# Split products from the sixth hidden block on, and low halves of w_out formed on GpSimd, in an attention and two-MLP kernel

## The chip, the cores and the metric

The kernel runs on one core of a Trainium2 chip. The number that counts is the device time of one execution in microseconds (us). Before the change three runs gave 1339.31, 1339.48 and 1341.15 us, so the median is 1339.48 us. Five engines work side by side: TensorE (PE in the profile, its weight loads PEld), VectorE (DVE), ScalarE (ACT), GpSimd (POOL) and SyncE (SP, which here only starts transfers).

## The reference

A small attention between 512 tokens and 32 state rows is computed in each of 8 batches and 8 heads. Its 4352 result rows of 512 values go through two MLPs, the first with a smooth step, the second with a sloped ReLU:

```
g  = where(h >= 1, h, where(h <= -1, 0, (h + 1)**2 / 4))   # h = x @ w_in,  512 -> 2048
x1 = g @ w_out                                             # 2048 -> 512
g2 = max(h2, 0) + alpha * min(h2, 0)                       # h2 = x1 @ w_in2
out = g2 @ w_out2
```

The weights arrive as 64-bit floats and are turned into 32-bit floats on the chip.

## The kernel before, in words

The first MLP runs over nine tiles of tokens: eight tiles of 512 tokens, one for each batch, and a last one of 256 state rows. Within a tile the 2048 hidden units are taken in 16 blocks of 128. A step `i` of the main loop stands for one tile and one block (step 0 to 15 is the first tile). It writes, in this order, the first layer of step i+2 (`h_mm`), the side work listed for that step in a table (`at(i, ...)`), the activation (`act_fn`, which forms `g`), the high and low half of the next step's `g` (`g_split`), and the second layer of step i (`out_mm`, four sums `accA` of 128x512). A scheduler then settles the order in which the instructions of each engine stand in the program.

A product of two 32-bit matrices is taken in one of two ways. In the whole form (line 602) it is one f32 matmul, which the trace shows as two passes. In the split form (line 610, and line 85 for the first layer, `hA`) both factors are cut into a high half, rounded to type `fp32r` by ScalarE (`hi_`, line 74), and the low rest, which VectorE forms by a subtraction (`lo_`, line 77). The product is then three fp32r matmuls: high by high, high by low and low by high. `NAT = 9` (line 100) says that steps 0 to 8 take their second layer in the whole form and all later steps in the split form.

The weight block `f` of w_out must therefore be there in the whole form by step f, and in two halves by the first step that uses the split form. `decode` turns 64-bit words into f32: one operation on ScalarE (`dec0`, line 372) and four on VectorE (`dec1`, lines 383 to 391). `dec_hi` makes the high half and `dec2` the low one; before the change blocks 9 to 15 get their halves in the first tile, blocks 0 to 8 only when the second tile comes to them.

During the first tile the program also prepares what the other tiles need. TensorE makes products of state and w_in in pairs of 64 rows each (`vg_mm`, line 481, `vgp`); ScalarE copies them out (`vgo`, line 484); GpSimd moves some of them to other partitions by DMA (`v0_move`, line 492) into `vr`, which ScalarE and VectorE split into `vw` for the first layer of the first tile; and GpSimd stores the decoded w_in in DRAM (`wi_store`, line 439, 64 transfers). VectorE also decodes w_in and does parts of the second batch's softmax. The PSUM tiles of `vgp`, of `hA` and of the attention scores come from one pool of four banks, so a `vgp` waits until an older tile of the pool has been read. All engines run their own instructions in the order in which they stand.

Of the kernel before, what the change touches and what calls it, by code (L numbers as in the profile page):

```python
# [40 lines left out]
def kernel_body(ctx: ExitStack, tc: tile.TileContext, x, state, w1i, w1o, w2i, w2o, alpha, out):  # L41
# [22 lines left out]
    act, dve, pool, pe, ld = nc.scalar, nc.vector, nc.gpsimd, nc.tensor, nc.sync  # L64
# [11 lines left out]
    def lo_(l, raw, h, eng=None):  # L76
        (eng or dve).tensor_tensor(out=l, in0=raw, in1=h.bitcast(F32), op=ALU.subtract)  # L77
# [19 lines left out]
    w2d = dp.tile([8, 7, 128, 512], F32, name="w2d")  # L97
    wd = [dp.tile([DM, 512], F32, name=f"wd{k}") for k in range(4)]
    GRP = [(1, 2, 3, 4), (0, 5, 6, 7)]
    NAT = 9  # L100


    A = {}
# [256 lines left out]
    G = {}  # L360
# [39 lines left out]

    def dec2(key):
        h, l = W[key]
        lo_(l, G.pop(("dec", key)), h)

    def decode(key, o):
        at(o - 1, dec0, key)
        at(o, dec1, key)
# [107 lines left out]
    def src_w1o(f):  # L515
        return w1o[f * 128:(f + 1) * 128, :]
# [20 lines left out]
    def gi(t, f):  # L537
        return t * NF + f
# [41 lines left out]
    def g_split(i):  # L580
        n = wd_(steps[i][0])
        g = GG.pop(i)
        if i < NAT:
            GH[i] = g
# [7 lines left out]
    def out_mm(i):  # L592
        t, f = steps[i]
        n = wd_(t)
        if f == 0:
            for k in range(NO):
                ACC[k] = pa.tile([128, 512], F32, tag="acc", name=f"accA{t}{k}")
        if i < NAT:

# [441 lines left out]
    def at(i, fn, *a):  # L1041
        side[i].append((fn, *a))
# [23 lines left out]
    for b in range(1, NB):  # L1066
        t0 = gi(b - 1, 0)
        for q in range(2):
            o = t0 + (2 if b > 1 else 5)
# [22 lines left out]
        for blk in range(4):  # L1092
            for q in range(2):
                o = t0 + 10 + 4 * blk + q
# [5 lines left out]
    for blk in (1, 2, 3):  # L1100
        for c in range(4):
            o = 4 * blk - 7 + c - (blk > 1)
# [2 lines left out]
            decode(("wi", blk, c), o)  # L1105
    at(1, vdirect, 0, 1)
    for f in range(1, NF):
        o = f - 2 - (f >= NAT)
        if f > 2:
            at(o - 3, d_load, ("w1o", f), src_w1o(f))  # L1110
        decode(("w1o", f), o)
    for f in range(NF):
        o = gi(1, f - 3) if f < NAT else f - 2
        at(o, dec_hi, ("w1o", f))
        at(o + 1, dec2, ("w1o", f))
    for n in range(4):
        at(n - 4, vg_mm, 1 - n % 2, 0, 2 + n // 2)
        at(n - 2, vg_store, 1 - n % 2, 0, 2 + n // 2)
# [1 line left out]
    for blk in range(4):  # L1120
        for c in range(4):
            if blk:
                o = 4 * blk - 3 + c
                at(o, vg_mm, 0, blk, c)
                at(o + 2, vg_store, 0, blk, c)
                o = 13 + c if blk < 2 else 4 * blk - 7 + c
# [142 lines left out]
```

## Time and profile before

| what | us |
|---|---|
| median of three runs (lowest, highest) | 1339.48 (1339.31, 1341.15) |
| profiled execution, its own time | 1339.59 |
| span of that execution in the trace | 1337.8 |
| TensorE busy in the span | 1327.5 |
| VectorE, ScalarE, GpSimd busy | 1025.7, 764.3, 186.9 |
| mean granted clock of TensorE | 0.999 of full speed |

The time of an execution is its span and a little around it, 1.8 us here. A busy time sums up what an engine did, and says nothing about who waited for whom at one place. That is read from the chain of waits, which is followed back from the last instruction, and from the instructions in order of time. Where a row of those carries a bracket, the engine was idle before it, and the bracket says for how long and what ended the wait. Durations of VectorE overlap a little with the next one: an operation of 0.69 us is followed by the next after 0.60 us.

### The profile page before, as it was taken

To read this page: it belongs to the slowest core of one execution; us is meant where nothing else is said; L and a number is where in the kernel's file an instruction comes from. 1 tells how busy PE (TensorE), PEld (TensorE's weight loads), DVE (VectorE), ACT (ScalarE), POOL (GpSimd) and SP (SyncE) were. 2 spreads that over 40 slices of the span, in tenths; PEclk is the share of its full clock that TensorE was granted. 3 is DMA by queue.
4 is the path that set the end of the run, shared out by engine and by line. 5 is a ranking of instruction groups with operands and counts; after the bars stand their busy time and mean duration, and the time that the engine had idled before them with its cause. 6 is when DMAs were issued, how large, how long until landed. Compare 5 with 4: busy or idle time off the path is not lost.

```text
span 1337.8 us, 21107 instructions
## 1 busy us (share of the span) xinstructions
PE 1327.5 (99%) x6962; PEld 1109.2 (83%) x6962; DVE 1025.7 (77%) x1868; ACT 764.3 (57%) x1500; POOL 186.9 (14%) x284
## 2 busy tenths in 40 slices
PE   9999999999999999999999999999999999999998
PEld 5335688878878888888988888888899999999998
DVE  6978575978697879776978696777868877796875
ACT  5757765666576666666745453554625445562543
POOL 1015400232323332223311000000000000000000
PEclk9999999999999999999999999999999999999999
DMA  8978862564666674465566865866688888969876
GB/s 278 328 268 235 244 144 66 129 191 125 205 157 191 172 233 141 144 227 174 204 221 221 283 205 173 266 186 212 212 269 265 285 273 299 310 209 298 272 255 191
DMA packets 262828, 293.03 MB, mean 219 GB/s; under 512 B 145152, under 2 KB 149824, under 8 KB 262720
## 3 DMA queue, kind: packets, MB, share of 16 engines
q1 hardware_dynamic: 243968, 247.73, 59.9%
q0 software_dynamic: 11904, 34.65, 7.3%
q10 hardware_dynamic: 6848, 9.31, 2.0%
q8 instruction: 56, 0.92, 0.3%
q14 instruction: 52, 0.43, 0.1%
HBM read 224.47 MB, written 66.06 MB: 217 GB/s over the span
## 4 chain that ended last, share of the span: by engine, by line
PE 92%; DVE 3%; issue 2%; ACT 2%; DMA 1%; POOL 1%; SPq 0%; ACTq 0%; DVEq 0%; POOLq 0%
PE accA L610 25%; PE accB L863 24%; PE hB L784 22%; PE hA L85 13%; PE accA L602 2%; PE vgp L481 2%; DMA x<-in_x_dram 1%; DMA vr<-vgo 1%; PE sr L253 1%; PE sc L159 1%; DVE c L810 0%; PE et L235 0%; ACT m L795 0%; DVE c L797 0%; ACT vgo L484 0%
## 5 line engine op out<-in xcount | busy, mean ns | idle before, releaser
L863 PE MATMUL accB<-gs,wv 128*128 128x384 f32 (+1 forms) x1668 | 331.4, 357 | 0.0
L863 PEld LDWEIGHTS accB<-gs,wv 128*128 128x128 f32 x1668 | 298.6, 188 | 27.6 <-DVE gs L77 1.9
L784 PE MATMUL hB<-xh,wu 128*128 128x384 f32 (+1 forms) x1120 | 314.7, 357 | 0.2 <-ACT p L814 0.2
L784 PEld LDWEIGHTS hB<-xh,wu 128*128 128x128 f32 x1120 | 205.8, 188 | 19.3 <-ACT p L814 1.4
L784 PE MATMUL hB<-xl,wu 128*128 128x384 f32 (+1 forms) x560 | 199.6, 356 | 0.0
L795 ACT ACTIVATE m<-c 128x384 f32<-128x384 f32 (+1 forms) x120 | 68.2, 568 | 140.4 <-DVE c L810 138.9
L578 DVE SCALAR_TENSOR_TENSOR g<-y,hA 128x512 f32<-128x512 f32 (+1 forms) x144 | 93.8, 651 | 56.2 <-ACT y L576 55.6
L77 DVE TENSOR_TENSOR gl<-g,gh 128x512 fp32r<-128x512 f32 (+1 forms) x135 | 95.1, 704 | 42.0 <-ACT gh L74 40.5
L797 DVE SCALAR_TENSOR_TENSOR c<-m,beta_sb,c 128x384 f32<-128x384 f32 (+1 forms) x120 | 80.9, 674 | 59.8 <-ACT m L795 56.2
L575 ACT ACTIVATE y<-hA 128x512 f32<-128x512 f32 (+1 forms) x144 | 82.7, 575 | 66.7 <-PE hA L85 66.6
L77 DVE TENSOR_TENSOR gs<-c,gs 128x384 fp32r<-128x384 f32 (+1 forms) x200 | 113.3, 604 | 6.9 <-ACT gs L845 6.4
L784 PEld LDWEIGHTS hB<-xl,wu 128*128 128x128 f32 x560 | 105.1, 188 | 8.7
L74 ACT CAST gh<-g 128x512 fp32r<-128x512 f32 (+1 forms) x135 | 80.3, 595 | 47.2 <-DVE g L578 39.1
L845 ACT CAST gs<-c 128x384 fp32r<-128x384 f32 (+1 forms) x200 | 101.6, 554 | 9.0 <-PE accB L863 8.6
L576 ACT ACTIVATE y<-y 128x512 f32<-128x512 f32 (+1 forms) x144 | 87.5, 608 | 3.8
L837 DVE TENSOR_TENSOR c<-c,c 128x384 f32<-128x384 f32 (+1 forms) x120 | 71.9, 608 | 2.1
L676 POOL DMA_DIRECT2D w2d<-wo x72 | 50.6, 904 | 132.0 <-DVE wo L77 66.0
L906 ACT COPY o<-accB 128x384 f32<-128x384 f32 (+1 forms) x30 | 15.7, 525 | 79.5 <-PE accB L863 77.3
L676 POOL DMA_DIRECT2D w1d<-wu x56 | 38.4, 753 | 149.6 <-DVE wu L77 122.9
L810 DVE TENSOR_TENSOR c<-hB,u 128x384 f32<-128x384 f32 (+1 forms) x80 | 48.4, 605 | 13.6 <-PE hB L784 11.7
L77 DVE TENSOR_TENSOR gs<-m,gs 128x384 fp32r<-128x384 f32 (+1 forms) x80 | 46.5, 607 | 12.4 <-ACT gs L845 12.4
L484 ACT COPY vgo<-vgp 128x512 f32<-128x512 f32 x64 | 34.3, 591 | 28.8 <-PE vgp L481 28.2
(905 smaller groups left out, 2662.0 us busy)
## 6 DMA issues: line engine op xcount, KB each, us to landing
wu<-w1d SPq DMA_DIRECT2D x280, 256.0 KB
wv<-w2d SPq DMA_DIRECT2D x280, 256.0 KB
vr<-vd SPq DMA_DIRECT2D x56, 256.0 KB
w1d<-wu POOLq DMA_DIRECT2D x56, 256.0 KB, 5.3
w2d<-wo POOLq DMA_DIRECT2D x40, 256.0 KB, 5.5
x<-in_x_dram SPq DMA_DIRECT2D x16, 512.0 KB
wr_wi<-in_moe_w_in_dram SPq DMA_DIRECT2D x16, 512.0 KB
wr_w1o<-in_moe_w_out_dram SPq DMA_DIRECT2D x16, 512.0 KB
```

What stands on the lines that cost most here:

```text
L74: act.copy(h, raw)
L77: (eng or dve).tensor_tensor(out=l, in0=raw, in1=h.bitcast(F32), op=ALU.subtract)
L85: pe.matmul(ps, a, b, start=(k == 0), stop=(k == n - 1))
L575: act.activation(out=y[:, :n], in_=ps, func=AF.Relu, bias=0.5, scale=0.5)
L576: act.activation(out=y[:, :n], in_=y[:, :n], func=AF.Square)
L578: dve.scalar_tensor_tensor(out=g[:, :n], in0=y[:, :n], scalar=1.0, in1=ps, op0=ALU.min, op1=ALU.max)
L610: pe.matmul(ACC[k][:, :n], a, b, start=(f == 0 and j == 0), stop=(f == NF - 1 and j == 2))
L676: pool.dma_start(out=dst, in_=src)
L784: pin(pe.matmul(ps, a[:, kk], b, start=(new and m == 0), stop=(m == 5), skip_group_check=True))
L797: dve.scalar_tensor_tensor(out=g, in0=m, scalar=beta_sb[:, f:f + 1], in1=h, op0=ALU.mult, op1=ALU.add)
L845: tc.keep_in_program_order(act.copy(h, src))
L863: pin(pe.matmul(ps, a[:, js], b, start=(new and k == 0 and n == 0), stop=(k == 7 and n == 2), skip_group_check=True))
```

## The change

There are three edits. `NAT` becomes 5, so that steps 5 to 8 of the first tile take their second layer in the split form, too. `dec2` gives its subtraction to GpSimd instead of VectorE, for all 16 blocks of w_out of the first MLP. And the table is moved so that the halves of blocks 5 to 8 are made in the first tile: the high half one step before the block is used, the low half in the same step. Blocks 9 to 15 keep their places.

```diff
-    NAT = 9
+    NAT = 5
     def dec2(key):
         h, l = W[key]
-        lo_(l, G.pop(("dec", key)), h)
+        lo_(l, G.pop(("dec", key)), h, pool)
     for f in range(1, NF):
-        o = f - 2 - (f >= NAT)
+        o = f - 2 - (f >= 9)
     for f in range(NF):
-        o = gi(1, f - 3) if f < NAT else f - 2
+        o = gi(1, f - 3) if f < NAT else f - 2 + (f < 9)
         at(o, dec_hi, ("w1o", f))
-        at(o + 1, dec2, ("w1o", f))
+        at(o + (f < NAT or f >= 9), dec2, ("w1o", f))
```

The order of the program changes on TensorE in steps 5 to 8 and at one pair of the second tile (eight transposes move by four products there, too). The first place is the end of block 5 in the first tile, on TensorE, before the change; `vgp` is the pair of 64-row products, `hA` the first layer, `accA` a sum of the second layer.

```order
L602 MATMUL accA_568<-g_739,wf_w1o_665 128x512
L602 MATMUL accA_569<-g_739,wf_w1o_665 128x512
L481 MATMUL vgp_887<-wf_wi_0_715,sts_223 128x512
L481 MATMUL vgp_888<-wf_wi_0_715,sts_223 128x512
L85 MATMUL hA_898<-ath_548,vw020h 128x512
L85 MATMUL hA_898<-atl_549,vw020h 128x512
```

The same place after the change, on TensorE:

```order
L610 MATMUL accA_569<-gl_801,w_w1o_5h 128x512
L610 MATMUL accA_569<-gh_800,w_w1o_5l 128x512
L481 MATMUL vgp_911<-wf_wi_0_715,sts_223 128x512
L610 MATMUL accA_566<-gh_878,w_w1o_6h 128x512
L610 MATMUL accA_566<-gl_879,w_w1o_6h 128x512
L481 MATMUL vgp_912<-wf_wi_0_715,sts_223 128x512
L85 MATMUL hA_922<-ath_548,vw020h 128x512
L85 MATMUL hA_922<-atl_549,vw020h 128x512
```

The pair of 64-row products no longer stands together: two products of the next block, the second of which needs the low half `gl_879`, stand between its members. From block 5 to block 8 four pairs stand apart in this way after the change (`vgp_868`, `vgp_911`, `vgp_941`, `vgp_993` and the product after each), and two before it (`vgp_856` and `vgp_913`).

The second place is block 0 of the second tile, on TensorE, before the change:

```order
L610 MATMUL accA_1564<-gh_1488,w_w1o_0l 128x512
L610 MATMUL accA_1565<-gh_1488,w_w1o_0h 128x512
L610 MATMUL accA_1565<-gl_1489,w_w1o_0h 128x512
L610 MATMUL accA_1565<-gh_1488,w_w1o_0l 128x512
L481 MATMUL vgp_1578<-wf_wi_3_502,sts_223 128x512
L481 MATMUL vgp_1579<-wf_wi_3_502,sts_223 128x512
```

The same place after the change, on TensorE:

```order
L610 MATMUL accA_1627<-gh_1552,w_w1o_0l 128x512
L481 MATMUL vgp_1642<-wf_wi_3_502,sts_223 128x512
L610 MATMUL accA_1628<-gh_1552,w_w1o_0h 128x512
L610 MATMUL accA_1628<-gl_1553,w_w1o_0h 128x512
L610 MATMUL accA_1628<-gh_1552,w_w1o_0l 128x512
L610 MATMUL accA_1629<-gh_1552,w_w1o_0h 128x512
L610 MATMUL accA_1629<-gl_1553,w_w1o_0h 128x512
L610 MATMUL accA_1629<-gh_1552,w_w1o_0l 128x512
L481 MATMUL vgp_1643<-wf_wi_3_502,sts_223 128x512
```

Here, too, one pair now stands apart, with six products between its members.

The third place is VectorE at the end of the decoding for step 6, before the change; `wf` is a decoded weight block, and the `g` written here frees the bank of an `hA`.

```order
L391 SCALAR_TENSOR_TENSOR wf_w1o_848<-wr_w1o_721,wf_w1o_848 128x512
L391 SCALAR_TENSOR_TENSOR wf_w1o_850<-wr_w1o_723,wf_w1o_850 128x512
L578 SCALAR_TENSOR_TENSOR g_868<-y_869,hA_827 128x512
L77 TENSOR_TENSOR vw021l<-vr_766,vw021h 128x512
L383 TENSOR_SCALAR wf_wi_3_905<-wf_wi_3_905 128x512
```

The same place after the change, on VectorE:

```order
L391 SCALAR_TENSOR_TENSOR wf_w1o_856<-wr_w1o_721,wf_w1o_856 128x512
L391 SCALAR_TENSOR_TENSOR wf_w1o_858<-wr_w1o_723,wf_w1o_858 128x512
L77 TENSOR_TENSOR gl_879<-g_807,gh_878 128x512
L578 SCALAR_TENSOR_TENSOR g_883<-y_884,hA_835 128x512
L77 TENSOR_TENSOR vw021l<-vr_766,vw021h 128x512
L383 TENSOR_SCALAR wf_wi_3_929<-wf_wi_3_929 128x512
```

The low half of block 6's `g` stands in front of the next `g`; blocks 5, 7 and 8 gain one such row each, and the 16 subtractions for w_out leave the engine. On GpSimd they stand between its transfers: those of blocks 5 to 9 between the moves into `vr`, that of block 10 behind the last move, those of blocks 11 to 15 and 0 to 4 between the 64 stores of w_in.

## Rows read from the trace of the kernel before

**Rows 1.** The page: busy time by engine, and granted clock in tenths by slice
```profile
PE 1327.5 (99%) x6962; PEld 1109.2 (83%) x6962; DVE 1025.7 (77%) x1868; ACT 764.3 (57%) x1500; POOL 186.9 (14%) x284
...
PEclk9999999999999999999999999999999999999999
```

**Rows 2.** Stretch 72 to 112: length, then PE, PEld, DVE, ACT, POOL busy
```profile
72.00:112.00 40.00, 39.67 (x120) 15.75 (x121) 34.91 (x73) 26.53 (x51) 4.98 (x10) 1.00 0.74 245
```

**Rows 3.** Chain of waits in order of time: start, length, what
```profile
57.15 3.63 PE accA L602 x8
...
80.51 1.05 PE vgp L481 x2
81.56 1.05 PE accA L602 x2
...
83.67 2.77 PE accA L602 x6
...
96.82 1.59 PE hA L85 x6
...
119.21 1.06 PE vgp L481 x4
120.27 2.93 PE accA L610 x12
123.20 1.36 PE hA L85 x6
...
135.32 2.72 PE accA L610 x12
```

**Rows 4.** TensorE in order of time: start, length, engine, line, tile, idle before
```profile
80.44 1.12 PE L481 MATMUL vgp<-wf_wi,sts 64*128 64x512 f32 x2
...
86.37 1.55 PE L481 MATMUL vgp<-wf_wi,sts 64*128 64x512 f32 x4
...
113.03 1.13 PE L481 MATMUL vgp<-wf_wi,sts 64*128 64x512 f32 x4
114.09 0.50 PE L610 MATMUL accA<-gh,w_w1o_9h 128*128 128x512 f32 x1
...
117.98 0.50 PE L85 MATMUL hA<-ath,vw031h 128*128 128x512 f32 x1 [0.21 <-ACT vw031h L74]
```

**Rows 5.** VectorE in order of time, same columns
```profile
78.44 0.69 DVE L391 SCALAR_TENSOR_TENSOR wf_w1o<-wr_w1o,wf_w1o 128x512 int32<-128x512 int32 x1
79.58 0.45 DVE L383 TENSOR_SCALAR wf_wi<-wf_wi 128x512 f32<-128x512 f32 x1 [0.45 <-ACT wf_wi L372]
...
86.06 0.68 DVE L578 SCALAR_TENSOR_TENSOR g<-y,hA 128x512 f32<-128x512 f32 x1
...
89.20 0.44 DVE L383 TENSOR_SCALAR wf_wi<-wf_wi 128x512 f32<-128x512 f32 x1 [1.86 <-ACT wf_wi L372]
...
102.64 0.68 DVE L578 SCALAR_TENSOR_TENSOR g<-y,hA 128x512 f32<-128x512 f32 x1
...
106.85 0.68 DVE L77 TENSOR_TENSOR w_w1o_9l<-wf_w1o,w_w1o_9h 128x512 fp32r<-128x512 f32 x1
...
110.78 0.68 DVE L578 SCALAR_TENSOR_TENSOR g<-y,hA 128x512 f32<-128x512 f32 x1
```

**Rows 6.** All engines in order of time around 374, in a later tile
```profile
374.38 3.12 DVE L77 TENSOR_TENSOR gl<-g,gh 128x512 fp32r<-128x512 f32 x1
...
374.54 1.02 POOL L654 TENSOR_TENSOR sao<-wf_w2o,wf_w2o 128x256 f32<-128x256 f32 x1
...
375.93 1.02 POOL L654 TENSOR_TENSOR sao<-sao,wf_w2o 128x256 f32<-128x256 f32 x1
```

**Rows 7.** All engines in order of time around 403
```profile
402.89 0.73 POOL L654 TENSOR_TENSOR sao<-sao,wf_w2o 128x256 f32<-128x256 f32 x1
...
403.04 1.13 DVE L77 TENSOR_TENSOR gl<-g,gh 128x512 fp32r<-128x512 f32 x1 [0.69 <-ACT gh L74]
```

**Rows 8.** Groups by line on GpSimd: count, busy and mean, idle before
```profile
L439 POOL DMA_DIRECT2D wd<-wf_wi x64 | 31.4, 498 | 13.3 <-DMA wd<-wf_wi 10.0 <-DVE gl L77 2.7 <-DMA vr<-vgo 0.6
```

## The prediction

> **What bounds the kernel now.** The page comes first: TensorE is busy for 99% of the span at a granted clock of full speed, all other engines for 77% or less [rows 1]. So a change pays only where it shortens TensorE's own work, or ends one of its few waits, and costs only where it makes TensorE wait. The second view is the busy time by stretch, for the time in which steps 5 to 8 run: in the 40 us from 72 to 112 TensorE idles for 0.3 us, and VectorE, with 34.91 us of work, is nearer to its limit than anywhere its 77% would suggest [rows 2]. The reader is to see that this stage has two full engines, not one. The third view is the chain of waits, which here runs along TensorE and so gives the price of each piece of its work, and the fourth is TensorE and VectorE in order of time, which shows who waits for whom.
>
> **Prices on TensorE.** A second-layer block in the whole form takes 3.63 us; in the split form 2.93 us behind a `vgp`, and 2.72 us, 0.227 a product, behind a first layer [rows 3]. The first layer takes 1.36 us behind split products and 1.59 behind a `vgp`. That is the arithmetic that speaks for the change: 3.63 - 2.93 = 0.70 for each of four blocks, 2.8 us. But a `vgp` pair takes 1.06 us, and half a pair that stands alone takes 1.05: the two halves run side by side, and a half alone saves nothing. Before the change two pairs are torn apart, by pieces of the second layer of 1.05 and 2.77 us [rows 3]; after it four are, and one more in the second tile.
>
> **Edit 1, split form in steps 5 to 8: TensorE's own work.** Before, from the lone `vgp` at 80.44 on: steps 5 and 6 take 1.05 + 1.05 + 1.05 + 2.77 + 1.06 + 1.59 = 8.57 us each, steps 7 and 8 take 1.06 + 3.63 + 1.06 + 1.59 = 7.34 each; the sum is 31.8 us. After, the same stretch holds 48 second-layer and 24 first-layer products at 0.227, 16.3 us, and 12 visits to `vgp` work (four pairs torn into eight, four whole). A visit among split products costs 1.06 and the 0.21 that the next split piece is longer behind it, 1.27; twelve cost 15.2 us. The sum is 31.6 us, so the gain on TensorE is 0.2 us instead of 2.8: the torn pairs have eaten the rest. The torn pair in the second tile costs 1.27 us. The rest of TensorE's order is that of before, and no term comes from it.
>
> **Waits that go.** The stretch from 80.44 to the `vgp` at 113.03 lasted 32.59 us [rows 4], 0.8 more than the 31.8 of work; the pair at 86.37 that took 1.55 instead of 1.06 shows most of it (its second half waits until a `g` has been read out of a bank, the `g` at 86.06 [rows 5]). And from 114.09 to 117.98 the second layer and half a first layer take 3.89 us where 2.93 + 3 x 0.227 = 3.6 were work: TensorE waits for the moved `vr` and its high half [rows 4], 0.3 us, and 0.3 more for its low half behind it. If TensorE comes to that place later, these 0.6 us go, too.
>
> **Edit 2, low halves on GpSimd: what it costs VectorE.** On VectorE such a subtraction takes 0.60 us of its time (the 0.68 us row at 106.85, the next starting 0.60 later [rows 5]). No row shows it on GpSimd at 128x512; at 128x256 a subtraction took 0.73 us undisturbed [rows 7], so at twice the width it takes between 0.73 and 1.46 us, and I take 1.3, near the row's cost per element. What it does to VectorE is the disputed price. Three GpSimd subtractions from 374.54 to 376.95 held a VectorE subtraction for 3.12 us instead of 0.69, 2.4 us longer; one at 402.89 held another for 1.13, 0.44 longer [rows 6, 7]. So VectorE stands still while GpSimd works, for 0.6 to 1 of the GpSimd time where it wants to work at once. For one low half of 1.3 us that is 0.8 to 1.3 us; where VectorE happens to be at work that GpSimd doesn't touch, it is nothing. It can't be a gain in steps 5 to 8, because only one subtraction leaves VectorE there, that of block 9. I take 0.9 us for each of the five low halves (blocks 5 to 9) that fall into the stage, and keep 0 and 1.3 as bounds.
>
> The Trainium skill (SBUF — State Buffer, "SBUF: two separate sides") says that the shared port pair of the two engines is an exclusive lock for a whole instruction, against VectorE operations with two SBUF inputs or in a two-port mode. The trace agrees with it in the 3.12 us row [rows 6]. By that rule the decode steps of this stage, nearly all of that kind, would be stopped for the whole low half, the upper bound. The same skill (GPSIMD Engine Reference, "3.1 Elementwise — side-by-side cycle accounting") gives about 2.6 cycles an element, from which I estimate 1.1 us and a start-up for 512 columns; with that the sum would stay within the range.
>
> **New waits on TensorE.** VectorE ended the decode before step 5's at 79.04, 0.54 us ahead of the next one, which began at 79.58 and ran without a break to the `g` at 86.06 [rows 5], 6.48 us. Now it has the low half of block 5's `g` (0.60) and the stop by w_out's block 5 (0.9) before that, and starts at 80.54; 6.48 and the stop by block 6 later, at 87.9, comes the low half of block 6's `g`, ready at 88.5, then the next `g`, ready at 89.1. TensorE gets there at 80.44 + 1.05 + 1.12 + 1.05 + 2.03 + 1.05 and one product = 87.1. It waits 1.4 us for the low half and 0.3 us for the bank that the `g` frees, in front of the second half of the torn pair. In steps 6 and 7 VectorE waits for decodes of ScalarE, as at 89.20 where it idled for 1.86 us [rows 5]; ScalarE does those behind the copies of the torn pair, so they come later by what TensorE is late, and VectorE wins back little. By the same count the `g` of block 9, which began at 102.64, is ready at 106.7, and the first layer of block 10 waits for its bank for 0.5 us. From that `g` to the next one VectorE needed 8.14 us before (102.64 to 110.78 [rows 5]); it loses block 9's subtraction (0.60), gains a reduction of the softmax that slips behind the `g` (0.60) and the stop by block 9 (0.9). The next `g` is ready at 115.75. TensorE stands at 114.3 then and could end its pair at 115.4; its second half starts at 115.8 and the pair ends at 116.85, 1.5 us late. New waits: 1.7 + 0.5 + 1.5 = 3.7 us.
>
> **The sum.** -0.2 (own work) - 0.8 and - 0.6 (old waits) + 3.7 (new waits) + 1.27 (torn pair in the second tile) = +3.4 us. What else moves costs nothing: the casts of blocks 5 to 8 on ScalarE are the same in number and lie in its idle time (26.5 of 40 us busy [rows 2]); if that cover were gone, the copies behind them and a `vgp` would come 0.5 us later each. In the second tile VectorE has nine subtractions fewer, but TensorE waits for none of them. The profiled execution took 1339.59 us, 1.79 above its span and 0.1 above the median; with 3.4 it gives 1343.0, and the median of 1339.48 gives 1342.9. I say 1342.8.
>
> **Rivals.**
>
> GpSimd doesn't hinder VectorE: stops of 0. For it speaks that in other stages operations of VectorE pass by GpSimd work unhurt; against it the two rows just used. Then VectorE is late by the 0.6 us of each low half of `g` alone, the waits of 3.7 shrink to 0.4 at the last pair, and the sum is -0.2 - 0.8 - 0.6 + 0.4 + 1.3 = +0.1: 1339.5 us, not slower. It decides below a stop of 0.2 us; at 0.5 the sum is +1.7.
>
> Torn pairs cost nothing: half a pair runs beside the products around it. Then two more torn pairs in the first tile and the one in the second cost about 0.2 us instead of 3.4, and with no stops the time falls by some 3.5 us, to 1336. The lone half at 80.51 that took 1.05 us speaks against it [rows 3].
>
> GpSimd's own queue is late. Eleven low halves (block 10 on) stand among or ahead of its 64 stores, 14 us of work where the queue had idled for 13.3 us, mostly for earlier stores to end [rows 8]. Each low half is behind a fixed number of stores (that of block 13 behind 23 of them, that of block 2 behind 54), and buffers that ScalarE and VectorE need are freed by those stores. I count a margin of 2 to 4 us for the tightest; should stores take 6 instead of 4 us each round because VectorE is in the way, TensorE waits once for 3 us more, on top of the forecast: 1346.
>
> **How the numbers follow.** The forecast has a chance of 0.50, no hindrance 0.27, torn pairs at no cost 0.04, a late queue 0.19. About 0.2% of the time, 2.7 us, is what a measurement can tell from no change. The forecast's own range goes from +1.7 (stops of 0.5) to +4.8 (1.3), 1341.2 to 1344.3, and three fifths of it lie above 2.7 us. Slower: 0.30 + 0.19, and a little more for what I haven't found, 0.50. The same: 0.20 + 0.25, 0.45. Faster: 0.05. The range is 1339.0 to 1346.0: it takes in the case without stops and the late queue, and leaves out the rival that is faster.
>
> **What would show it.** Right: on TensorE, waits in front of the product with `gl` of block 6, of the second half of that torn pair, and of the second half of the pair ahead of block 9, released by VectorE; decode operations of VectorE of 1.3 us and more beside a low half on GpSimd; three more lone `vgp` halves of 1.05 us; everything behind 165 us moved by a constant. Wrong: low halves on GpSimd with VectorE's operations at their usual 0.42 and 0.69 us; a TensorE without waits from 80 to 120; or waits released by GpSimd, which would be the queue. The size would be wrong if a low half on GpSimd took under 0.8 us or over 1.6.

## The result

The change makes the kernel slower by 0.64%: six runs of the changed kernel had a median of 1346.76 us (1345.96 to 1352.43), six of the kernel before 1339.72 (1338.29 to 1342.02), the ratio is 1.0064 with a 95% interval of 1.0052 to 1.0076. The prediction was 1342.8 us, slower, with a range to 1346.0. The direction was right; the loss is about twice what was forecast. The profiled execution took 1345.99 us over a span of 1344.2, 6.4 us more than that of before.

Where these 6.4 us lie is read from TensorE's instructions in order of time, at five marks that both kernels have: the first `vgp` of step 5, the first products with blocks 9 and 10 of w_out in the first tile, and those with blocks 0 and 1 in the second.

| TensorE | before, us | after, us | difference | forecast |
|---|---|---|---|---|
| start to `vgp` of step 5 | 80.44 | 81.12 | +0.7 | 0 |
| steps 5 to 8, up to block 9's product | 33.65 | 37.39 | +3.7 | +2.7 |
| block 9's to block 10's product | 6.11 | 7.05 | +0.9 | -0.6 |
| block 10's to block 0's product | 31.07 | 31.06 | 0.0 | 0 |
| block 0's to block 1's product | 5.38 | 6.66 | +1.3 | +1.3 |
| from there to the end | 1181.2 | 1180.9 | -0.2 | 0 |

(The forecast's +2.7 is made of -0.2 own work, -0.8 of an old wait and +3.7 of new ones.)

### The profile page after: what moved, and what is told of

Read it like the earlier page. It is cut to its first block, busy times and chain, and to the rows that moved or that the text cites. A ratio compares the mean times of both kernels' runs of the same rounds, so it can differ in the third digit from the quotient of the medians.

```text
span 1344.2 us, 21197 instructions
## 1 busy us (share of the span) xinstructions
PE 1329.9 (99%) x6978; PEld 1113.3 (83%) x6978; DVE 1030.9 (77%) x1856; ACT 766.1 (57%) x1504; POOL 208.6 (16%) x300
## 4 chain that ended last, share of the span: by engine, by line
PE 89%; DVE 5%; issue 2%; ACT 2%; DMA 1%; POOL 1%; SPq 0%; ACTq 0%; DVEq 0%; POOLq 0%
PE accA L610 25%; PE accB L863 24%; PE hB L784 22%; PE hA L85 12%; PE vgp L481 1%; PE accA L602 1%; DMA vr<-vgo 1%; PE sr L253 1%; DMA x<-in_x_dram 0%; DVE c L810 0%; PE et L235 0%; PE sc L159 0%; DVE wf_w1o L388 0%; ACT m L795 0%; DVE c L797 0%
## 5 line engine op out<-in xcount | busy, mean ns | idle before, releaser
L77 DVE TENSOR_TENSOR gl<-g,gh 128x512 fp32r<-128x512 f32 (+1 forms) x139 | 100.4, 722 | 45.6 <-ACT gh L74 44.2
```

## The profile after

The page's first part and the stretch from 72 to 112 us, which answer to [rows 1, 2]; the columns are the same.

```profile
PE 1329.9 (99%) x6978; PEld 1113.3 (83%) x6978; DVE 1030.9 (77%) x1856; ACT 766.1 (57%) x1504; POOL 208.6 (16%) x300
```

```profile
72.00:112.00 40.00, 37.04 (x126) 17.52 (x127) 36.44 (x64) 27.97 (x54) 12.53 (x15) 1.00 0.67 228
```

The page's first part could be taken for that of before: shares of 99 and 77% again. The stretch can't. TensorE, which idled for 0.3 us there, now idles for 3.0, and VectorE, with fewer instructions in the same 40 us than before (64 for 73), is busy for longer (36.44 for 34.91 us). An instruction takes it 0.57 us in the mean instead of 0.48.

GpSimd and VectorE of the changed kernel in order of time say why (start, length, engine, line, tile, idle before). First GpSimd:

```profile
74.69 1.46 POOL L77 TENSOR_TENSOR w_w1o_5l<-wf_w1o,w_w1o_5h 128x512 fp32r<-128x512 f32 x1 [0.95 <-ACT w_w1o_5h L74]
...
93.46 1.84 POOL L77 TENSOR_TENSOR w_w1o_7l<-wf_w1o,w_w1o_7h 128x512 fp32r<-128x512 f32 x1 [0.93 <-ACT w_w1o_7h L74]
...
116.51 1.43 POOL L77 TENSOR_TENSOR w_w1o_10l<-wf_w1o,w_w1o_10h 128x512 fp32r<-128x512 f32 x1
117.88 2.96 POOL L439 DMA_DIRECT2D wd<-wf_wi  x6
120.85 1.41 POOL L77 TENSOR_TENSOR w_w1o_11l<-wf_w1o,w_w1o_11h 128x512 fp32r<-128x512 f32 x1
```

Then VectorE:

```profile
74.62 0.42 DVE L385 TENSOR_SCALAR wf_wi<-wf_wi 128x512 int32<-128x512 int32 x1
74.95 1.49 DVE L385 TENSOR_SCALAR wf_w1o<-wf_w1o 128x512 int32<-128x512 int32 x1
...
88.67 0.68 DVE L77 TENSOR_TENSOR gl<-g,gh 128x512 fp32r<-128x512 f32 x1
...
94.08 1.50 DVE L385 TENSOR_SCALAR wf_w1o<-wf_w1o 128x512 int32<-128x512 int32 x1
...
116.72 0.68 DVE L578 SCALAR_TENSOR_TENSOR g<-y,hA 128x512 f32<-128x512 f32 x1
117.32 0.90 DVE L383 TENSOR_SCALAR wf_w1o<-wf_w1o 128x512 f32<-128x512 f32 x1
...
119.45 1.67 DVE L391 SCALAR_TENSOR_TENSOR wf_w1o<-wr_w1o,wf_w1o 128x512 int32<-128x512 int32 x1
121.04 1.78 DVE L77 TENSOR_TENSOR gl<-g,gh 128x512 fp32r<-128x512 f32 x1
122.74 0.67 DVE L578 SCALAR_TENSOR_TENSOR g<-y,hA 128x512 f32<-128x512 f32 x1
123.33 0.68 DVE L77 TENSOR_TENSOR vw031l<-vr,vw031h 128x512 fp32r<-128x512 f32 x1
```

The two operations of line 385 at 74.62 and 74.95 are the same work; the second, beside a subtraction of GpSimd, takes 1.49 us instead of 0.42, a stop of 1.07. The same is seen beside block 7 (1.50, a stop of 1.08). Beside blocks 6, 8 and 9 one operation each time was longer by 1.0, 1.0 and 1.4 us. Beside block 10 it is 0.48 (0.90 for 0.42), and the `g` at 116.72, one of whose operands is in PSUM, isn't stopped at all. Beside block 11 two operations are stopped, by 1.0 and 1.1 us (1.67 and 1.78 against 0.69); the first lies ahead of the row of GpSimd's subtraction, whose times are rough.

TensorE in order of time, which answers to [rows 4]:

```profile
89.40 0.49 PE L610 MATMUL accA<-gl,w_w1o_6h 128*128 128x512 f32 x1 [1.47 <-DVE gl L77]
...
107.95 0.50 PE L85 MATMUL hA<-ath,vw020h 128*128 128x512 f32 x1 [0.70 <-DVE g L578]
...
115.74 1.12 PE L481 MATMUL vgp<-wf_wi,sts 64*128 64x512 f32 x2
117.46 1.12 PE L481 MATMUL vgp<-wf_wi,sts 64*128 64x512 f32 x2 [0.60 <-DVE g L578]
118.51 0.50 PE L610 MATMUL accA<-gh,w_w1o_9h 128*128 128x512 f32 x1
...
124.07 0.50 PE L85 MATMUL hA<-ath,vw031l 128*128 128x512 f32 x1 [1.41 <-DVE vw031l L77]
```

The first three waits are those the prediction named: `gl` of block 6 (forecast 1.4, measured 1.47), the bank for the first layer of block 10 (0.5, 0.70), and the pair ahead of block 9, which takes 2.77 us (115.74 to 118.51) instead of 1.06, so 1.7 late where 1.5 was forecast: 0.60 us of waiting, and then the second half takes its 1.05 us alone, no longer beside the first. The fourth wasn't forecast: instead of losing 0.6 us of old waits at `vw031`, TensorE waits 1.41 us for its low half.

## The experiments

Two theories stood. A: GpSimd's subtractions stop VectorE, and TensorE waits for the late VectorE. B: the torn pairs and VectorE's extra `gl` cost the time, and GpSimd is harmless. In the table, "steps 5 to 8", "9 to 10" and "0 to 1" are the stretches of TensorE named above, from each kernel's profile; ratios are to the kernel before, on the same chip.

| kernel | median, us | ratio (95%) | steps 5 to 8 | 9 to 10 | 0 to 1 |
|---|---|---|---|---|---|
| before (trace) | 1339.72 | | 33.65 | 6.11 | 5.38 |
| changed | 1346.76 | 1.0064 (1.0052, 1.0076) | 37.39 | 7.05 | 6.66 |
| e1 low halves on VectorE | 1341.32 | 1.0011 (1.0003, 1.0020) | 33.72 | 6.00 | 6.66 |
| e2 low halves on GpSimd, split from 9 | 1343.13 | 1.0020 (1.0012, 1.0029) | 33.66 | 7.41 | 5.38 |
| e3 pairs whole | 1347.84 | 1.0063 (1.0048, 1.0077) | 38.66 | 6.98 | 6.54 |
| e4 blocks 0 to 4 on GpSimd | 1342.06 | 1.0011 (1.0003, 1.0020) | 34.30 | 5.99 | 6.66 |
| e5 VectorE, pairs whole | 1339.65 | 1.0000 (0.9988, 1.0011) | 33.35 | 5.75 | 7.11 |
| e6 VectorE, last pair whole | 1341.44 | 1.0009 (0.9999, 1.0019) | 34.30 | 6.00 | 5.57 |
| e7 blocks 10, 11 on VectorE | 1346.96 | 1.0057 (1.0043, 1.0070) | 40.25 | 5.39 | 6.66 |
| e8 blocks 5 to 9 on VectorE | 1345.04 | 1.0039 (1.0023, 1.0055) | 34.33 | 8.98 | 6.66 |
| e9 spare subtractions | 1351.29 | 1.0080 (1.0061, 1.0099) | 44.53 | 8.22 | 6.65 |
| e10 spare copies | 1342.55 | 1.0034 (1.0013, 1.0055) | 35.38 | 5.99 | 7.76 |
| e11 before, pairs whole | 1341.34 | 1.0017 (1.0008, 1.0027) | 34.87 | 5.72 | 5.38 |

Falls of TensorE's clock, told below, lie in "steps 5 to 8" of e3, e7 and e9 and around block 10's product in e8; e1 and e11 had one ahead of step 5, outside the three stretches.

**e1: the split form alone (`NAT` and the table, low halves on VectorE).**

```diff
-        lo_(l, G.pop(("dec", key)), h, pool)
+        lo_(l, G.pop(("dec", key)), h)
```

> The changed kernel with the low halves of w_out back on VectorE (edit 1 alone). Theory A (GpSimd's subtractions stop VectorE, about 1.07 us each for 0.60 us of work saved, and the late VectorE makes TensorE wait): the stops go, the five low halves cost VectorE 0.60 us each instead, and TensorE's waits between 72 and 125 us fall from 5.0 to between 2 and 3 us; the time is 1343.5, 2.5 to 3 us under the changed kernel's 1346.0 to 1346.8, still 4 above before, with the torn pair of the second tile (1.27) in it. Theory B (the torn pairs and the extra VectorE work are what costs, GpSimd is harmless): VectorE has 0.60 us more for each block, so the time is that of the changed kernel or up to 1 us more, 1346 to 1348.

Steps 5 to 8 take 33.72 us, as before the change, and TensorE's waits between 72 and 126 us are 1.7 us instead of 5.0. The wait for `vw031l` is 0.35 us, where the changed kernel had 1.41:

```profile
120.58 0.50 PE L85 MATMUL hA<-ath,vw031l 128*128 128x512 f32 x1 [0.35 <-DVE vw031l L77]
```

The time is 1341.32, 5.4 us under the changed kernel and 2 us lower than theory A had said. B is out: VectorE has more instructions here and TensorE waits less. Of its 0.11% over before, the second tile's block is 1.3 us.

**e2: low halves on GpSimd alone.** The kernel before (`NAT = 9`) with `pool` in `dec2`.

> The kernel before with the low halves of w_out on GpSimd (edit 2 alone; split form from block 9 on as before). TensorE's order is that of before, no pair is torn anew. Theory A: the subtractions of blocks 9 to 11 stop VectorE for 1 us and more each ahead of the low half of the moved weights (vw031l), and the wait there is 1 us longer than before; the time is 1340.5 to 1341.5, 1 to 2 us above before. Theory B: nothing waits for VectorE there for long, the time is that of before within 0.3 us.

TensorE in front of the low half:

```profile
119.89 0.49 PE L85 MATMUL hA<-ath,vw031l 128*128 128x512 f32 x1 [1.19 <-DVE vw031l L77]
```

The trace shows the wait for `vw031l` as 1.19 us and the stretch from block 9 to 10 as 1.3 longer, as A had it; the medians differ by 3.1 us, more than the 1 to 2 expected. The split form and the move to GpSimd cost 0.11 and 0.20% alone, 0.64 together: they are not additive. The first reason lies in the program. With `NAT = 9` the halves of blocks 5 to 8 are not made in the first tile, so of GpSimd's subtractions only block 9's (at 106.23) falls into steps 5 to 8; the split form brings four more. And that one stop (two operations of 0.69 us took 2.55 together) did not reach TensorE here: steps 5 to 8 took 33.66 us.

**e3: the changed kernel with its pairs whole.** Each second-layer product of steps 5 to 8 and 16, and the first half of the torn pair of the second tile, is pinned to its written place:

```diff
-                pe.matmul(ACC[k][:, :n], a, b, start=...)
+                ins = pe.matmul(ACC[k][:, :n], a, b, start=...)
+                if i < 9 or i == 16:
+                    tc.keep_in_program_order(ins)
```

> The changed kernel with every pair of vgp products kept together (the order of TensorE pinned in steps 5 to 8 and in block 0 of the second tile; low halves stay on GpSimd). Theory A: in steps 5 to 8 VectorE sets the pace, so what TensorE saves on four torn pairs (4 x 1.27 = 5 us) comes back as longer waits for gl and g in the main; only the 1.27 us of the second tile are sure, and 0 to 1.5 more: 1343.5 to 1345. Theory B: all five torn pairs are given back, 6.3 us: 1339.7, no slower than before.

Nothing came back, not even the 1.27 us of the second tile (6.54 us for 6.66; there the whole pair takes 2.08 us, its second half waiting for its bank). In steps 5 to 8 TensorE now stands idle in front of three second halves, twice 0.68 us for a copy `vgo` and once 1.94 for a `g`, and for 2.34 us of another `g` in front of the pair ahead of block 9. (The 5.0 and 2.3 us that the text on e5 gives for these waits are sums over the whole execution.) Worse than A had it, since such a wait has a second price. TensorE in order of time:

```profile
118.71 1.13 PE L481 MATMUL vgp<-wf_wi,sts 64*128 64x512 f32 x4 [2.34 <-DVE g L580]
119.77 0.69 PE L612 MATMUL accA<-gh,w_w1o_9h 128*128 128x512 f32 x1
120.26 0.63 PE L612 MATMUL accA<-gl,w_w1o_9h 128*128 128x512 f32 x1
120.68 0.63 PE L612 MATMUL accA<-gh,w_w1o_9l 128*128 128x512 f32 x1
```

The products behind the wait come every 0.42 to 0.49 us instead of 0.23, and the granted clock of 120 to 124 is 0.58; from 96 to 100 it was 0.57. So the 38.66 us are not the waits alone.

**e4: only blocks 0 to 4 on GpSimd.**

```diff
-        lo_(l, G.pop(("dec", key)), h, pool)
+        lo_(l, G.pop(("dec", key)), h, pool if key[1] < NAT else None)
```

> The changed kernel with only the low halves of blocks 0 to 4 on GpSimd (they run after 140 us, where TensorE waits for nobody), and those of blocks 5 to 15 on VectorE. Theory A: stops after 140 us are free, and the time is that of the run with all low halves on VectorE within 0.4 us, 1343.5. Theory B: as the changed kernel, 1346 or more. A third reading, that GpSimd's late queue (its stores) is what costs: then this is 1 us and more faster or slower than the run with all on VectorE.

The same as e1, within what can be told (1342.06 and 1341.32, the same ratio). What GpSimd's low halves after 140 us cost is too little to be told.

**e5 and e6: low halves on VectorE, with all pairs whole, and with only that of the second tile whole** (e1's edit, with the pins of e3; for e6 only those of `i == 16` and of that pair).

> Split form from block 5 on, low halves on VectorE, all vgp pairs whole. With the low halves on GpSimd whole pairs gained nothing: TensorE stood in front of the second half of a pair for 5.0 us of g and 2.3 us of vgo instead. Theory A' (a pair is torn because its bank is late, and the products between its halves cover that wait): without GpSimd's stops VectorE is earlier, so the waits at the pairs are shorter than with GpSimd but still eat most of the 5 us; from the first vgp of step 5 to the first product with block 9 TensorE takes 32.5 to 34 us (33.72 with the pairs torn, 33.65 before), time 1340.5 to 1342. Theory B (a torn pair is a cost of its own): 29 us there and 5.38 instead of 6.66 us in block 0 of the second tile, time 1335.5.

> Low halves on VectorE, and only the pair in block 0 of the second tile kept whole. If that pair's 1.27 us is the price of its being torn, block 0 of the second tile takes 5.4 us instead of 6.66 and the time falls to 1340.0. If the pair is torn because ScalarE frees its bank late (the copies vgo stand behind those of oA), the block stays at 6.3 to 6.7 us and the time at 1341.3.

In e5 steps 5 to 8 gain 0.4 us, not 5. TensorE at the first of its whole pairs:

```profile
81.12 1.12 PE L481 MATMUL vgp<-wf_wi,sts 64*128 64x512 f32 x2
82.92 1.12 PE L481 MATMUL vgp<-wf_wi,sts 64*128 64x512 f32 x2 [0.68 <-ACT vgo L486]
83.97 0.50 PE L612 MATMUL accA<-gh,w_w1o_5h 128*128 128x512 f32 x1
```

This pair takes 2.85 us and not 1.06: its second half waits, and then it can't run beside the first any more. Three of the four pairs that were torn go that way, with waits of 0.68, 0.65 and 0.68 us, 2.85, 2.82 and 2.85 us in all; that is 1.8 us each, more than the 1.27 that a tear costs. The time equals that of before, although block 0 of the second tile is longer here than with its pair torn (7.11, with 0.61 us of wait for `vgo`). In e6 that block does shrink, to 5.57, but the time stays at e1's. So what the tear of this pair cost was 1.1 us in one profile (e6) and 0.1 us or nothing in two (e3, e5). The split form by itself, with its pairs whole, is worth nothing here, and no kernel of this study beats the one before.

**e7 and e8: which stops cost where.**

```diff
-        lo_(l, G.pop(("dec", key)), h, pool)
+        lo_(l, G.pop(("dec", key)), h, None if key[1] in (10, 11) else pool)     # e7
+        lo_(l, G.pop(("dec", key)), h, None if 5 <= key[1] <= 9 else pool)       # e8
```

> The changed kernel with the low halves of blocks 10 and 11 alone on VectorE. Theory A (the stops by GpSimd's low halves of blocks 10 and 11, 0.5 and 2.1 us, make vw031l late, the step that the prediction had as a gain): the wait for vw031l falls from 1.41 to under 0.7 us, the stretch from the first product with block 9 to that with block 10 goes from 7.05 back to 6.0 to 6.3 us, and steps 5 to 8 keep their 37.4; the time is 0.8 to 1 us under the changed kernel's, 1345.1 in an execution without a fall of the clock. Rival (VectorE is late there from steps 5 to 8 and would be late anyhow): the stretch stays at 7 us.

> The changed kernel with the low halves of blocks 5 to 9 alone on VectorE; those of blocks 10 to 15 and 0 to 4 stay on GpSimd. Theory A (the stops of blocks 5 to 9 make TensorE wait in steps 5 to 8): from the first vgp of step 5 to the first product with block 9 33.7 to 34.5 us instead of 37.39; the wait for vw031l stays over 1 us, as it was 1.19 with edit 2 alone; time 1342.0 to 1343. Rival (the low halves of block 10 on, or the stores behind them, are what costs): that stretch stays over 36 us, time over 1344.5.

VectorE of e7 in order of time:

```profile
118.61 0.68 DVE L578 SCALAR_TENSOR_TENSOR g<-y,hA 128x512 f32<-128x512 f32 x1
...
121.45 0.69 DVE L391 SCALAR_TENSOR_TENSOR wf_w1o<-wr_w1o,wf_w1o 128x512 int32<-128x512 int32 x1
122.06 0.68 DVE L77 TENSOR_TENSOR gl<-g,gh 128x512 fp32r<-128x512 f32 x1
122.81 0.69 DVE L578 SCALAR_TENSOR_TENSOR g<-y,hA 128x512 f32<-128x512 f32 x1
123.41 0.68 DVE L77 TENSOR_TENSOR vw031l<-vr,vw031h 128x512 fp32r<-128x512 f32 x1
```

From this `g` to `vw031l` VectorE takes 4.80 us, with the low half of block 10 among its own work; in the changed kernel it was 6.61 (116.72 to 123.33). In both kernels that `g` frees the bank of the pair ahead of block 9, so TensorE's way to `vw031` begins with it, too. The 1.8 us are the stops of blocks 10 and 11 less that low half, and the wait for `vw031l` is gone: 5.39 us for 7.05. The rival is out. The median shows none of it (1346.96), nor could it in this profile: steps 5 to 8 took 40.25 us, since behind the same 1.47 us of wait for `gl` of block 6 the clock fell (0.57 from 88 to 96 us).

e8 takes steps 5 to 8 back to 34.33 us, as A said, and loses part of it at once: TensorE comes to `vw031` earlier and waits 2.87 us for its low half, which the stops of blocks 10 and 11 keep late.

```profile
122.41 0.50 PE L85 MATMUL hA<-ath,vw031l 128*128 128x512 f32 x1 [2.87 <-DVE vw031l L77]
```

Behind that wait the clock fell (0.65 from 124 to 128), which made the way to block 0 of the second tile 1.2 us longer than in the changed kernel. Its time, 1345.04, is 2 us over what was expected. Only both groups together (e1, e4) give nearly all of the loss back.

**e9 and e10: interference or dependence.** As e1, and GpSimd works beside it on a spare tile that nobody reads:

```diff
-        lo_(l, G.pop(("dec", key)), h)
+        raw = G.pop(("dec", key))
+        lo_(spare, raw, h, pool)              # e10: pool.tensor_copy(spare, raw)
+        lo_(l, raw, h)
```

> Split form from block 5 on, all low halves on VectorE, and beside them GpSimd makes the same 16 subtractions once more into a spare tile (16-bit, 128x512) that nobody reads, at about the places where the changed kernel had them. No engine waits for a result of GpSimd's, so this tells interference from dependence. Theory A (GpSimd's subtraction stops VectorE while it runs): VectorE's neighbours last 1.4 to 1.9 us as in the changed kernel, and, with the low halves on VectorE as well, the time is that of the changed kernel or more, 1345.5 to 1348; from the first vgp of step 5 to the first product with block 9 37 us or more. Rival (late results of GpSimd, or its queue, are what costs): the time of the kernel with the low halves on VectorE, 1341 to 1342, that stretch 33.7 us.

> As the run with spare subtractions, but GpSimd only copies the decoded block into the spare tile: one operand from SBUF instead of two. If any work of GpSimd stops VectorE, it is as slow as the spare subtractions, 1345 or more. If the stop hangs on the two operands, VectorE's operations keep 0.42 and 0.69 us beside the copies, and the time is 1341 to 1342. I expect the second with 6 in 10.

In e9 no engine needs what GpSimd's subtractions make, and it is the slowest kernel of all, 3 us above the top of what was expected. GpSimd, then VectorE in order of time:

```profile
74.95 1.49 POOL L77 TENSOR_TENSOR spare<-wf_w1o,w_w1o_5h 128x512 bf16<-128x512 f32 x1 [0.93 <-ACT w_w1o_5h L74]
```

```profile
75.23 1.76 DVE L77 TENSOR_TENSOR w_w1o_5l<-wf_w1o,w_w1o_5h 128x512 fp32r<-128x512 f32 x1
...
82.49 1.40 DVE L386 TENSOR_SCALAR wf_wi<-wf_wi 128x512 int32<-128x512 int32 x1
```

So it is interference. The 44.5 us of steps 5 to 8 are not stops alone: the clock fell there for 12 us (below).

In e10 the copies are short, 0.74 us in the mean, and stand earlier than e9's subtractions, as they don't need the high half. The time can't be told from e1's (the intervals overlap; nine runs spread from 1340 to 1350), but in the profile steps 5 to 8 are 1.7 us longer than e1's, 0.86 of it a wait for the `gl` of block 6. The expectation that a copy doesn't stop VectorE was wrong. GpSimd, then VectorE of e10 in order of time:

```profile
90.53 0.62 POOL L405 CAST spare<-wf_w1o 128x512 bf16<-128x512 f32 x1
...
103.62 0.61 POOL L405 CAST spare<-wf_w1o 128x512 bf16<-128x512 f32 x1 [2.77 <-DVE wf_w1o L392]
```

```profile
90.34 1.10 DVE L384 TENSOR_SCALAR wf_wi<-wf_wi 128x512 f32<-128x512 f32 x1 [1.19 <-ACT wf_wi L373]
...
103.73 1.05 DVE L77 TENSOR_TENSOR gl<-g,gh 128x512 fp32r<-128x512 f32 x1 [0.24 <-ACT gh L74]
...
112.09 0.69 DVE L77 TENSOR_TENSOR gl<-g,gh 128x512 fp32r<-128x512 f32 x1
```

Beside a copy of 0.62 us a decode step takes 1.10 us instead of 0.42, and beside one of 0.61 a `gl` takes 1.05 instead of 0.69: a copy stops VectorE, too, here for 0.7 and 0.4 us.

**e11: the kernel before with its pairs whole** (e3's pin on the second-layer products, those of line 602 from step 5 on as well).

> The kernel before, whole form up to block 8, with its two torn vgp pairs (steps 5 and 6) kept whole. If a torn pair costs about 1 us of TensorE, from the first vgp of step 5 to the first product with block 9 it takes 31.5 us instead of 33.65, and the time is 1337.5. If the tear only covers the wait for a bank, 33.0 to 33.8 us there and 1339 to 1340, no difference.

Steps 5 to 8 take 34.87 us for 33.65, with three waits of 0.67 or 0.68 us for `vgo`, two of them in front of second halves, and the time is 0.17% over before; neither forecast had that. Tearing these pairs is a gain.

## Why the prediction was half right

**The mechanism** was right: GpSimd stops VectorE, VectorE is late, and TensorE waits at the three places named. The rival without hindrance is ruled out by e1 and e9. The late queue is, too: no wait of TensorE in the changed kernel ends with GpSimd, all of the new ones end with VectorE or ScalarE, and no wait of those two ends with a store of w_in. The low half on GpSimd took 1.29 to 1.84 us (1.3 forecast), the stops of blocks 5 to 9 were 1.0 to 1.4 us (0.9 forecast), and the three waits were 1.47, 0.70 and 1.7 (1.4 and 0.3 for a bank behind it, 0.5, and 1.5 forecast).

**The step that failed** is "If TensorE comes to that place later, these 0.6 us go, too." It counted TensorE's lateness and not VectorE's. The stops were counted for blocks 5 to 9 and ended there, though the subtractions of blocks 10 and 11 stand on GpSimd right behind, next to the `gl` and `g` ahead of `vw031l`. The -0.6 became +0.9, half of the 3 us by which the sum fell short. e7 shows it: those two on VectorE, and the wait is gone. e8 shows it from the other side: with only blocks 10 to 15 and 0 to 4 on GpSimd the wait is 2.87 us.

**Steps 5 to 8** were 1.0 us longer than the sum. The three waits were mis-sized by only 0.2 in total (1.47, 0.70 and 1.7 for 1.7, 0.5 and 1.5); the other 0.8 lie in TensorE's own pieces around them, and which of these grew stays open. The start was 0.7 late, which the forecast had as 0. Of this 0.4 have a reason outside the change, mostly a wait at 72 us, 0.24 before and 0.56 after, for the copies behind a transfer into `vr`, ahead of GpSimd's first subtraction; it was 0.79 in e1, 0.97 in e4 and none in e10. The other 0.2 are a wait for a `g` of VectorE ahead of the scores `sc`, at 80.09; only the kernels in which GpSimd subtracts block 5's halves have it (0.16 to 0.18 us in the changed kernel, e3, e7 and e9), so it goes with block 5's stop, and the sum had left it out.

**The torn pairs** were priced well as TensorE's own time: up to block 9's product the prediction's prices give 31.6 + 1.06 = 32.7 us, and e1, with 0.8 us of waits in it, took 33.72. With this the rival in which torn pairs cost nothing is out. But "the torn pairs have eaten the rest" sounds as if whole pairs would give the rest back, and they don't. e3, e5 and e11 kept pairs whole in three kernels, and steps 5 to 8 went from 37.39 to 38.66 (with falls of the clock), 33.72 to 33.35 and 33.65 to 34.87. The second half's bank isn't free yet, the products between the halves fill that wait, and a pair whose second half waits takes 2.85 us. In e5 two of these banks were freed by copies of ScalarE and one by a `g` of VectorE, in e11 both by copies. The 2.8 us of the split form couldn't be had either way here.

**The last part of the miss** is the clock, for which the sum had no term. Three of the six runs were within 0.04 us of 1345.99; the others, at mean clocks of 0.998 to 0.994, took 1347.5 to 1352.4 and raised the median by 0.8 us.

## What to carry to other kernels

Work moved from a busy VectorE to an idle GpSimd isn't free: here a subtraction mostly cost VectorE 1.0 to 1.4 us of standing still to save it 0.60. Move it only where nobody waits for VectorE (blocks 0 to 4 here), and count the stops on to the next thing that is waited for, not to the end of the stage that was edited. An instruction that the scheduler has put between the halves of a pair may be covering a wait; look at when the second half's buffer is free before calling the gap a loss that can be won back.

## What the runs showed of the hardware

A wait of TensorE can cost more than its length. Stretches of e9 (length, then PE, PEld, DVE, ACT, POOL busy, granted clock, DMA share, GB/s):

```profile
84.00:88.00 4.00, 4.00 (x13) 1.91 (x11) 4.00 (x10) 2.92 (x6) 0.00 (x0) 1.00 0.51 200
88.00:92.00 4.00, 2.06 (x4) 0.69 (x3) 3.90 (x7) 0.41 (x1) 0.51 (x1) 0.80 0.23 68
92.00:104.00 12.00, 12.00 (x21) 5.80 (x20) 6.75 (x11) 5.05 (x9) 2.25 (x2) 0.50 0.40 131
104.00:108.00 4.00, 4.00 (x13) 1.82 (x11) 2.73 (x8) 1.36 (x3) 0.51 (x1) 0.99 0.21 66
```

TensorE idled for 1.94 us here, and then stood at 0.50 of full speed, 1.2 GHz, for 12 us, which by these rows cost an estimated 6 us of its work, although it was busy throughout. In the changed kernel a wait of 1.47 us at the same place had no such fall, and in e7 one of the same 1.47 us had (0.57 over 8 us). Nor does it take GpSimd's subtractions: ahead of step 5 the clock stood at 0.50 from 74 to 76 us in e1 behind a wait of 0.79 us, while e4 had none behind 0.97. What decides in a given run isn't settled.

GpSimd's stop of VectorE doesn't need two operands: operations with one (0.42 us alone) and with two (0.69) were both stopped for about a microsecond, while the `g` at 116.72, which takes one of its two from PSUM, was not. By the Trainium skill (SBUF — State Buffer, "SBUF: two separate sides") whoever of the two engines starts first holds the shared ports for the whole instruction. The rows agree roughly in the length: a stop of 1.07 us beside an instruction of 1.46, of 0.7 and 0.4 beside the copies of 0.62 and 0.61 in e10. But the two operations stopped beside block 11's subtraction lost 2.1 us to one of 1.41. Nor do the rows show the order: the decode step at 90.34 in e10 begins before its copy (90.53), the one at 119.45 in the changed kernel 1.4 us before its subtraction (120.85), and both were stopped. As GpSimd's times are rough, no run here settles who came first.
